# Dealing out DVE work and summing v in longer bursts in a windowed-attention and Fourier-mixing kernel

## The chip, the cores and the metric

The kernel runs on one core of one Trainium2 chip. The time is device time of one execution in microseconds; the time before is the median of three executions. One further execution was profiled, and all rows of a profile come from that one. The core has a matrix engine (TensorE, PE in the profile, with its weight loads as PEld), a vector engine (VectorE, DVE), a scalar engine (ScalarE, ACT), GpSimd (POOL), and the queue SP (SyncE), which issues nearly all DMAs here. Each engine takes its own instructions in order and waits for the others by semaphores.

## The reference

```python
g = sigmoid((x * gate_w).sum(-1))                  # x: 2048 x 512
a = x @ dft_hid_re.T;  b = x @ dft_hid_im.T        # 512 x 512 each
y = dft_seq_re @ a - dft_seq_im @ b                # 2048 x 2048 each
q, k, v = heads(x @ wqkv)                          # 32 heads of 16
p = softmax(mask(q @ k.T / 4))                     # 0 <= i - j < 256
out = g * y + (1 - g) * ((p @ v) @ wo)
```

All inputs and outputs are float32. There are two branches over the same 2048 rows: a Fourier mixing, which is dense matmuls alone, and an attention in which each row sees the 256 rows up to itself. A gate per row mixes the two.

## The kernel before

**Dense stream.** A generator, `dense`, yields one matmul of 512 columns at a time: the projections to q and k (`qk_proj`, four groups `g` of heads, rows named `dqk`), to v (`v_proj`, `dv`) and to the Fourier branch (`ab_proj`, `dab`), then the large products with `cr` and `ci` (`c_part`, L446, `dc`), last the product with `wo` (L669). Every dense operand is kept as a high and a low part in the type float32r, and each product is three matmuls (`TERMS`: high by high, high by low, low by high). Twelve matmuls make one projected tile. An operand is split by `split`: L80 copies the high part, L81 subtracts it for the low part. `split_raw` does this for a whole weight, in four DVE operations of 512 columns one behind the other. A tile that a projection made is split as it leaves PSUM (L84 on ACT, L86 or L88 on DVE) into a tile `hl`, of which there are three, and stored to `qk_scr` or `ab_scr` in HBM.

**Attention.** 128 blocks of 64 rows (4 groups of heads by 32), each with four pairs of heads `p`. `s_pair` makes the scores of block n (L325), DVE adds the mask and finds the minimum of the negated scores (L327), ACT takes the exponentials only for their sum `l` (L330). 20 blocks later (`LAG`) `t_pair` makes the transposed scores of block k = n - 20 with the maxima built in (L388), ACT writes their exponentials into a tile `pt` (L389; four tiles), GpSimd cuts the edges of the window (L394, L398), and `pv` sums v with them (L415, rows named `o`, float32, 32 columns of the array for each pair). The maxima and the sums of 8 blocks are turned from columns to rows by `ml_rows`: one matmul with a float32 identity (L337), then DVE work (L340 to L344) and small DMAs; `m_ring` loads the maxima back. `make_pad` (L308, L310) writes the block's weights. `v_load` and `v_spread` bring v for four blocks at a time into one of two `vpad` tiles (L378 on GpSimd).

**Order.** The order on TensorE is written out by hand in the last loop: for each block and pair a score matmul, dense matmuls, a transposed score matmul, dense matmuls. `fill` adds to a quota and takes that many from the dense stream, which gives 4 x `FILL` dense matmuls per block: 12 for the first 20 blocks (`FILL_FIRST` 3.0), 14 while there are projections left (`FILL_PROJ` 3.5), 14.4 later (`FILL_SEQ` 3.6). Every third block, behind pair 2, `pv` is called for three blocks at once (a burst), and `ml_rows` behind it when eight blocks of sums are complete. On the other engines a scheduler sets the order from its own estimate; `behind` keeps an instruction behind the last one marked on the named engines, and `late` does so for ACT and DVE.

**Buffers.** PSUM has four banks for `s`, `t` and the turned rows (`ps_a`), two for `o`, two for dense products. Raw weights and rows of x have two tiles `raw`, their splits three each of `hi` and `lo`; a load into a tile waits on SP, with every later DMA of that queue behind it.

**End.** After the loop `attention_done` loads and splits `wo`. The rest of the dense stream follows, with the products of `wo` between blocks of 48 `dc` matmuls; `wo_prep` loads and splits (`os`, L78 and L81) the attention's output for them.

## Time and profile before

| | before |
|---|---|
| median of 3 runs | 869.55 us (868.85 to 870.48) |
| profiled execution, whole | 873.39 us |
| its span, first to last instruction | 871.3 us |
| TensorE busy | 860.5 us, 99% |
| DVE busy | 611.3 us, 70% |
| ACT busy | 580.9 us, 67% |
| POOL busy | 384.6 us, 44% |
| granted TensorE clock, mean | 0.998 |
| DMA | 157.87 MB, mean 181 GB/s |

Engine rows of the page give busy time, share of the span and the number of instructions. The chain is the work that ended last, followed back from the last instruction. A row of the timeline has its start, its length, the engine, the line, and what it writes and reads, with shapes and count; in square brackets the idle time before it and what ended that. A matmul's length holds a tail that the next one overlaps, so the rate is read from one start to the next. A row of the waits has the engine and its line, the one waited for, the total in us, the count and the longest. A group of instructions has its busy time, the mean of one in ns, and the idle time before. Busy time by stretch has the stretch, its length, and for PE, PEld, DVE, ACT and POOL the busy time with the number of instructions.

### The profile page before, as it was taken

The page shows a single profiled execution, that of the slowest core. Times are in us where ns is not written, and L with a number is a line of the kernel's source. Part 1 is how long each engine was busy: PE and PEld are TensorE (multiplying, and loading weights), DVE is VectorE, ACT ScalarE, POOL GpSimd, SP SyncE. Part 2 cuts the span into 40 slices and gives each one's busy share as a digit, 9 for nine tenths or more (in the row PEclk, how much of TensorE's full clock was granted, in tenths as well). Part 3 has the DMA queues.
Part 4 walks back from the last instruction along what each step waited for, and adds up shares of the span by engine and source line. Part 5 has one row for each costly group of instructions (what it writes and reads, how often), then busy time and mean ns, then how long its engine had stood idle before and what let it go on. Part 6 is the DMA issues. An engine that isn't in the chain of part 4 may idle for free.

```text
span 871.3 us, 17146 instructions
## 1 busy us (share of the span) xinstructions
PE 860.5 (99%) x5160; PEld 690.3 (79%) x5160; DVE 611.3 (70%) x1974; ACT 580.9 (67%) x1793; POOL 384.6 (44%) x1067
## 2 busy tenths in 40 slices
PE   8999999999999999999999999999999999999998
PEld 6888778787877778878788887878778787788886
DVE  4588987667878987878787777788876444564431
ACT  4388799888897987878788777877776454111110
POOL 9100054545444756656456566554546665200000
PEclk9999999999999999999999999999999999999999
DMA  6875796464749436644445354599944333485541
GB/s 229 266 226 155 248 262 197 153 214 158 241 158 289 130 105 225 172 130 135 134 131 170 105 163 133 156 349 256 329 148 159 123 118 114 130 263 192 189 145 48
DMA packets 93132, 157.87 MB, mean 181 GB/s; under 512 B 27120, under 2 KB 36080, under 8 KB 93040
## 3 DMA queue, kind: packets, MB, share of 16 engines
q1 hardware_dynamic: 92288, 155.61, 56.5%
q10 hardware_dynamic: 752, 1.18, 0.4%
q8 instruction: 40, 0.66, 0.3%
q14 instruction: 52, 0.43, 0.2%
HBM read 106.69 MB, written 50.07 MB: 180 GB/s over the span
## 4 chain that ended last, share of the span: by engine, by line
PE 92%; DVE 3%; DMA 2%; ACT 1%; issue 1%; SPq 0%; DVEq 0%; ACTq 0%
PE dc L446 40%; PE dab L266 9%; PE s L325 8%; PE o L415 8%; PE dqk L244 8%; PE t L388 8%; PE t L669 5%; PE dv L266 4%; DVE sm L327 1%; PE s L232 1%; DMA raw<-x 1%; ACT sm L330 1%; DMA ring<-qk_scr 1%; PE s L337 1%; DMA pt<-xT 0%
## 5 line engine op out<-in xcount | busy, mean ns | idle before, releaser
L446 PE MATMUL dc<-big,hi 128*128 128x512 f32 x1024 | 355.4, 395 | 0.0
L394 POOL TENSOR_SCALAR_AFFINE_SELECT pt<-pt 64x128 f32<-64x128 f32 x512 | 191.9, 375 | 276.4 <-ACT pt L389 261.2
L330 ACT ACTIVATE sm<-sm,ml 128x320 f32<-128x320 f32 (+4 forms) x512 | 277.3, 543 | 49.4 <-DVE ml L327 48.0
L327 DVE CUSTOM_DVE_ANT_0 sm<-s,mask 128x320 f32<-128x320 f32 (+4 forms) x512 | 230.7, 462 | 82.7 <-PE s L325 62.5
L389 ACT ACTIVATE pt<-t 128x320 f32<-128x320 f32 (+4 forms) x512 | 208.7, 412 | 89.8 <-PE t L388 86.2
L446 PEld LDWEIGHTS dc<-big,hi 128*128 128x128 f32 x1024 | 186.3, 188 | 32.6 <-issue 2.4
L446 PE MATMUL dc<-big,lo 128*128 128x512 f32 x512 | 201.6, 394 | 0.0
L398 POOL TENSOR_SCALAR_AFFINE_SELECT pt<-pt 64x128 f32<-64x128 f32 x448 | 161.9, 361 | 0.1
L325 PE MATMUL s<-ring,pad 128*128 128x320 f32 (+4 forms) x512 | 159.0, 310 | 0.9 <-DVE ml L327 0.5
L388 PE MATMUL t<-ring,pad 128*128 128x320 f32 (+4 forms) x512 | 155.1, 303 | 1.6 <-DVE ml L327 0.9
L310 DVE TENSOR_SCALAR pad<-ring,half 96x256 fp32r<-96x256 f32 x384 | 121.6, 358 | 24.2 <-PE t L388 22.0
L325 PEld LDWEIGHTS s<-ring,pad 128*128 128x128 f32 x512 | 96.0, 188 | 36.6 <-issue 7.4
L388 PEld LDWEIGHTS t<-ring,pad 128*128 128x128 f32 x512 | 96.1, 188 | 21.6 <-DVE ml L327 2.6
L446 PEld LDWEIGHTS dc<-big,lo 128*128 128x128 f32 x512 | 96.3, 188 | 10.6
L81 DVE TENSOR_TENSOR lo<-raw,hi 128x512 fp32r<-128x512 f32 x146 | 99.6, 712 | 1.4 <-PE dc L446 1.3
L330 ACT ACTIVATION_READ_ACCUMULATOR sm<-sm,ml 128x1 f32 x512 | 98.8, 193 | 0.0
L266 PE MATMUL dab<-hi,big 128*128 128x512 f32 x256 | 90.9, 396 | 0.0
L244 PE MATMUL dqk<-big,hi 128*128 128x512 f32 x240 | 86.7, 394 | 0.6 <-DVE hl L86 0.5
L80 DVE CAST hi<-raw 128x512 fp32r<-128x512 f32 x142 | 58.6, 453 | 38.3 <-PE dc L446 37.1
L415 PE MATMUL o<-pt,vpad 128*32 128x320 f32 (+4 forms) x1408 | 73.8, 351 | 0.0
L378 POOL COPY vpad<-vr 64x256 f32<-64x256 f32 x64 | 26.0, 405 | 91.1 <-DMA vr<-v_scr 72.0
L308 ACT ACTIVATE pad<-ring,half 96x256 fp32r<-96x256 f32 x128 | 64.1, 500 | 0.0
(82 smaller groups left out, 780.3 us busy)
## 6 DMA issues: line engine op xcount, KB each, us to landing
qk_scr<-hl SPq DMA_DIRECT2D x32, 512.0 KB
ring<-qk_scr SPq DMA_DIRECT2D x32, 512.0 KB
raw<-cr SPq DMA_DIRECT2D x32, 512.0 KB
raw<-ci SPq DMA_DIRECT2D x32, 512.0 KB
ab_scr<-hl SPq DMA_DIRECT2D x20, 512.0 KB
big<-ab_scr SPq DMA_DIRECT2D x20, 512.0 KB
r_scr<-ev SPq DMA_DIRECT2D x36, 256.0 KB
ev<-r_scr SPq DMA_DIRECT2D x36, 256.0 KB
```

Source lines behind the costliest of these rows:

```text
L244: nc.tensor.matmul(ps, w[a][:, c:c + 128], XT[dk, ss][:, b], start=n == 0, stop=n == 11)
L266: nc.tensor.matmul(ps, XT[dk, ss][:, a, c * 128:(c + 1) * 128], wh[b], start=n == 0, stop=n == 11)
L310: nc.vector.tensor_scalar(dst, src, half[:96, h:h + 1], None, op0=OP.mult)
L325: nc.tensor.matmul(ps[:, :w], PAD[0, n][:, p], ring[1][:, p, k0:k0 + w], start=True, stop=True)
L327: mark("dve", nc.vector.tensor_tensor_reduce(out=sm[:, :w], in0=ps[:, :w], in1=mask[:, WIN - w:], scale=1.0, scalar=3e38, op0=OP.add, op1= ...
L330: mark("act", nc.scalar.activation(sm[:, :w], sm[:, :w], AF.Exp, bias=nm[:, c], scale=-1.0, accum_out=l[:, c]))
L388: nc.tensor.matmul(ps[:, :w], PAD[1, n][:, p], ring[0][:, p, q0:q0 + w], start=True, stop=True)
L389: nc.scalar.activation(pt[:, p, :w], ps[:, :w], AF.Exp, scale=-1.0)
L394: nc.gpsimd.affine_select(a, a, pattern=[[0, 2], [1, 64]], compare_op=OP.is_ge, fill=0.0, base=0, channel_multiplier=-1)
L398: nc.gpsimd.affine_select(a, a, pattern=[[0, 2], [-1, 64]], compare_op=OP.is_gt, fill=0.0, base=0, channel_multiplier=1)
L415: nc.tensor.matmul(OT[g, sb][32 * p:32 * p + 32, q - sb * 512:e - sb * 512], v2[:, p], pt[:, p, q - q0:e - q0], start=first, stop=kb == 8 ...
L446: nc.tensor.matmul(ps, w[a][:, i % 8 * 128:i % 8 * 128 + 128], ab[SC[i]][:, b], start=i == ends[0] and a + b == 0, stop=i == ends[1] and a ...
```

## The change

Six things are changed.

- `FILL_PROJ` goes from 3.5 to 4.0 and `FILL_SEQ` from 3.6 to 3.8: 16 and 15.2 dense matmuls per block.
- Weight splits (`split_soon`), the splits of x (`x_job`) and the gate products are put on a list `jobs`. `job`, called behind every matmul of a projection, takes one from it at the third and the ninth of its twelve matmuls. The splits of `cr`, `ci` and `wo` stay as they were. Several loads of raw weights move with the splits that free their tiles.
- Once all projections are through, the sums of v go in bursts of five blocks. The tiles `hl` have grown to the size of a `pt` and serve as two more of these (`more`), so there are six; there are two `hl` where there were three.
- v is spread as soon as the sums that read the older `vpad` are issued, in the burst, and the load for the next four blocks follows (`v_next`).
- Turning: `ml_split` splits maxima and reciprocal sums in a high and a low part, `ml_turn` turns both with two float32r matmuls (the identity is float32r now) two blocks later, `ml_rows` takes them on a pair later, `m_ring` three blocks after that. A table, `TURN`, has their places.
- The last loop is one block shorter (`N + LAG + 1`), and the last sums are taken when k reaches N.

```diff
@@ -26,7 +26,7 @@
...
 SWITCH = 4
-FILL_FIRST, FILL_PROJ, FILL_SEQ = 3.0, 3.5, 3.6
+FILL_FIRST, FILL_PROJ, FILL_SEQ = 3.0, 4.0, 3.8
 @with_exitstack
@@ -100,6 +100,20 @@
...
         return hi, lo
+    jobs = []
+    def split_soon(raw):
+        hi = st.tile([P, 1024], F32R, name="hi")
+        lo = st.tile([P, 1024], F32R, name="lo")
+        for c in HALVES:
+            jobs.append(lambda c=c: late(nc.vector.tensor_copy, hi[:, c], raw[:, c]))
+            jobs.append(lambda c=c: late(nc.vector.tensor_sub, lo[:, c], raw[:, c], f(hi[:, c])))
+        return hi, lo
+    def job(n):
+        if n % 6 == 3 and jobs:
+            jobs.pop(0)()
     def load_split(src, act=False):
@@ -154,9 +168,9 @@
...
                                 base=256, channel_multiplier=1)
-    ident = const.tile([P, P], F32, name="ident")
-    nc.gpsimd.memset(ident, 1.0)
-    nc.gpsimd.affine_select(ident, ident, pattern=[[1, P]], compare_op=OP.is_equal, fill=0.0,
+    ident = const.tile([P, P], F32R, name="ident")
+    nc.gpsimd.memset(f(ident[:]), 1.0)
+    nc.gpsimd.affine_select(ident[:], f(ident[:]), pattern=[[1, P]], compare_op=OP.is_equal, fill=0.0,
                             base=0, channel_multiplier=-1)
@@ -218,8 +232,12 @@
     TERMS = ((0, 0), (0, 1), (1, 0))
+    def hl_tile():
+        t = ev.tile([P, NP, WIN], F32R, name="hl", bufs=2)
+        return t.rearrange("p a b -> p (a b)")[:, :1024].rearrange("p (h s) -> p h s", h=2)
     def qk_evict(g, ss, i, ps):
-        hl = ev.tile([P, 2, 512], F32R, name="hl", bufs=3)
+        hl = hl_tile()
         split_psum(hl[:, 0], hl[:, 1], ps, -SCALE if i == 0 else 1.0)
@@ -244,6 +262,7 @@
...
                     n += 1
+                    job(n)
                     if n < 12:
@@ -266,6 +285,7 @@
...
                 n += 1
+                job(n)
                 if n < 12:
@@ -286,7 +306,7 @@
...
         if dst is None:
-            hl = ev.tile([P, 2, 512], F32R, name="hl", bufs=3)
+            hl = hl_tile()
             split_psum(hl[:, 0], hl[:, 1], ps, 1.0 if i == 0 else -1.0)
@@ -311,6 +331,8 @@
...
     ML = {}
+    MH = {}
+    MT = {}
     def s_pair(n, p):
@@ -330,22 +352,35 @@
...
                                          accum_out=l[:, c]))
+    def ml_split(u):
+        ml = ML.pop(u).rearrange("p x c -> p (x c)")
+        MH[u] = at.tile([P, 2, NP * 16], F32R, name="mlh", bufs=1)
+        with behind("dve"):
+            nc.vector.reciprocal(ml[:, 32:], ml[:, 32:])
+            nc.vector.tensor_copy(MH[u][:, 0], ml)
+            mark("dve", nc.vector.tensor_sub(MH[u][:, 1], ml, f(MH[u][:, 0])))
+    def ml_turn(u):
+        hl = MH.pop(u)
+        MT[u] = ps_a.tile([P, 512], F32, name="s", tag="st")
+        for h in range(2):
+            nc.tensor.matmul(MT[u][:64, h * P:h * P + P], hl[:, h], ident, start=True, stop=True)
     def ml_rows(u):
-        ml = ML.pop(u)
-        nc.vector.reciprocal(ml[:, 1], ml[:, 1])
-        pt = ps_a.tile([P, 512], F32, name="s", tag="st")
-        nc.tensor.matmul(pt[:64, :P], ml.rearrange("p x c -> p (x c)"), ident, start=True, stop=True)
-        hl = at.tile([32, 2, 2, 64], F32R, name="mhl", bufs=1)
-        m = pt[:32, :P].rearrange("c (a r) -> c a r", a=2)
-        nc.vector.tensor_scalar(hl[:, :, 0], m, -1.0, None, op0=OP.mult)
-        nc.vector.scalar_tensor_tensor(hl[:, :, 1], m, -1.0, f(hl[:, :, 0]), op0=OP.mult, op1=OP.subtract)
-        ld(m_scr[u].rearrange("x p (j r) -> (p j) x r", r=64), f(hl[:]).rearrange("c a h r -> c (a h) r"))
-        lt = at.tile([64, P], F32, name="lt", bufs=1)
-        nc.vector.tensor_copy(lt[32:64], pt[32:64, :P])
+        pt = MT.pop(u)
+        rows = at.tile([64, 2 * P], F32R, name="mhl", bufs=1)
+        hl = rows[:32].rearrange("c (a h r) -> c a h r", a=2, h=2)
+        lt = f(rows[32:64, :P])
+        m = pt[:32, :2 * P].rearrange("c (h a r) -> c h a r", h=2, a=2)
+        with behind("dve"):
+            nc.vector.tensor_scalar(hl.rearrange("c a h r -> c h a r"), m, -1.0, None, op0=OP.mult)
+            nc.vector.tensor_copy(lt, pt[32:64, :P])
+            mark("dve", nc.vector.tensor_add(lt, pt[32:64, P:2 * P], lt))
+        ld(m_scr[u].rearrange("x p (j r) -> (p j) x r", r=64), f(hl).rearrange("c a h r -> c (a h) r"))
         for a in range(2):
...
             ld(bass.AP(tensor=ls.tensor, offset=ls.offset + a * 512, ap=[[1024, NP], [64, 8], [1, 64]]),
-               lt[32:64, 64 * a:64 * a + 64])
+               lt[:, 64 * a:64 * a + 64])
     def m_ring(u):
@@ -355,6 +390,7 @@
...
     PT = {}
+    more = []
     VR = {}
@@ -382,7 +418,12 @@
...
         if p == 0:
-            PT[n] = at.tile([P, NP, WIN], F32, name="pt", bufs=4)
+            if "proj" in have:
+                more.append(n)
+            if more and (n - more[0]) % 6 < 2:
+                PT[n] = f(ev.tile([P, NP, WIN], F32R, name="hl", bufs=2)[:])
+            else:
+                PT[n] = at.tile([P, NP, WIN], F32, name="pt", bufs=4)
         pt = PT[n]
@@ -492,24 +533,28 @@
...
         yield
+        def x_job(ss, dk):
+            late(split_x, ss, (dk,), ss == 1)
+            if dk % 2 and ss < 3:
+                load_x(ss + 1, dk // 2)
         for ss in range(4):
+            if ss < 3:
+                for dk in range(DK):
+                    jobs.append(lambda ss=ss, dk=dk: x_job(ss + 1, dk))
+                    jobs.append(lambda: None)
             if ss:
                 yield from qk_proj(0, ss, wq0)
+            if ss == 3:
+                w = split_soon(raw)
             for c in range(4):
...
                     have.add(("qk", 0, ss))
-                if ss < 3:
-                    if c in (1, 2):
-                        late(split_x, ss + 1, (2 * c - 2, 2 * c - 1), ss == 0)
-                        if ss < 2:
-                            load_x(ss + 2, c - 1)
-                elif c == 0:
+                if ss == 2 and c == 2:
                     raw = load_raw(wqk[1])
                     wraw = [load_raw(wi[0])]
-                elif c == 2:
-                    w = late(split_raw, raw)
         for g in range(1, NG):
@@ -517,28 +562,27 @@
...
                         wraw.append(load_raw(wi[1]))
-                    elif ss < 3:
-                        if ss == 1:
-                            ws = []
-                        ws.append(late(split_raw, wraw[ss - 1]))
-                        if ss == 1:
-                            raw = load_raw(wqk[2])
+                        ws = [split_soon(wraw[0])]
+                    elif ss == 1:
+                        ws.append(split_soon(wraw[1]))
+                        raw = load_raw(wqk[2])
                 elif g == 2:
...
                         wraw = [load_raw(wr[0])]
+                    elif ss == 1:
+                        nextw = split_soon(raw)
                     elif ss == 2:
-                        nextw = late(split_raw, raw)
                         wraw.append(load_raw(wr[1]))
-                elif ss in (0, 2):
-                    if ss == 0:
-                        ws = []
-                    ws.append(late(split_raw, wraw[ss // 2]))
+                elif ss == 0:
+                    ws = [split_soon(wraw[0])]
+                elif ss == 1:
+                    ws.append(split_soon(wraw[1]))
             if g == 1:
...
                     if sb == 1:
-                        nextw = late(split_raw, raw)
+                        nextw = split_soon(raw)
             if g < 3:
@@ -550,8 +594,7 @@
...
                 if sb > 1:
-                    late(gate, 2 * sb - 4)
-                    late(gate, 2 * sb - 3)
+                    jobs.extend([lambda tb=tb: late(gate, tb) for tb in (2 * sb - 4, 2 * sb - 3)])
         for sc in range(4):
@@ -703,13 +746,21 @@
...
     N = NG * NB
-    maxima = sent = 0
-    taken = []
+    TURN = (8, 1, ml_split), (10, 0, ml_turn), (10, 1, ml_rows), (13, 0, m_ring)
     need(("qk", 0, 0))
...
     need(("v", 5))
-    for n in range(N + LAG + 2):
+    summed, spread = 0, 2
+    def v_next(n):
+        if n < N:
+            for c in range(2):
+                need(("v", n % NB // 2 + c))
+            with behind(*(("sp",) if n < 8 else ())):
+                v_load(n)
+    for n in range(N + LAG + 1):
         if n in (1, 3, 5):
@@ -717,13 +768,12 @@
...
         ring_ahead(n + 1)
-        if -4 <= k < N - 4 and k % 4 == 0:
-            for c in range(2):
-                need(("v", (k + 4) % NB // 2 + c))
-            with behind(*(("sp",) if k < 4 else ())):
-                v_load(k + 4)
-        if -4 <= k and k % 4 == 3:
+        if k in (-4, 0):
+            v_next(k + 4)
+        if k in (-1, 3):
             v_spread(k + 1)
+        if k == 3:
+            v_next(8)
         if n == 0:
@@ -737,17 +787,18 @@
...
             fill(n)
-            if p == 2 and sent < maxima and n >= taken[sent] + 2:
-                m_ring(sent)
-                sent += 1
-            if p == 2 and k % 3 == 0:
-                for j in range(k - 3, k):
-                    if 0 <= j < N:
-                        pv(j)
-                if maxima < 16 and n > 8 * maxima + 8:
-                    ml_rows(maxima)
-                    maxima += 1
-                    taken.append(n)
+            for at_n, at_p, do in TURN:
+                u, j = divmod(n - at_n, 8)
+                if p == at_p and j == 0 and 0 <= u < 16:
+                    do(u)
+            if p == 2 and (k - summed >= (5 if more else 3) or k == N):
+                for j in range(summed, k):
+                    pv(j)
+                summed = k
+                while 4 * spread - 5 < summed and 4 * spread < N:
+                    v_spread(4 * spread)
+                    spread += 1
+                    v_next(4 * spread)
     attention_done()
```

## The prediction

> **What bounds the kernel now.** I read the page first (engines, then the chain that ended last), then the chain in order of time, then the timeline of TensorE in short stretches, the waits, and busy time by stretch.
>
> ```profile
> span 871.3 us, 17146 instructions
> PE 860.5 (99%) x5160; PEld 690.3 (79%) x5160; DVE 611.3 (70%) x1974; ACT 580.9 (67%) x1793; POOL 384.6 (44%) x1067
> ...
> PE 92%; DVE 3%; DMA 2%; ACT 1%; issue 1%; SPq 0%; DVEq 0%; ACTq 0%
> ```
>
> TensorE is busy for 99% of the span and carries 92% of the chain. So time can be won only where a matmul takes longer than its share of a dense stream, and lost only where TensorE starts to wait. The page's means cannot give that share, since neighbouring matmuls overlap; starts can.
>
> ```profile
> 758.84 21.12 PE dc L446 x92
> 779.96 10.99 PE t L669 x48
> ...
> 812.82 10.88 PE dc L446 x48
> ```
>
> 48 matmuls of 512 columns in 10.88 us are 0.227 us each.
>
> ```profile
> 353.71 0.31 PE L325 MATMUL s<-ring,pad 128*128 128x320 f32 x1
> 353.86 0.40 PE L446 MATMUL dc<-big,hi 128*128 128x512 f32 x1
> ...
> 354.47 0.39 PE L446 MATMUL dc<-big,hi 128*128 128x512 f32 x1
> 354.80 1.84 PE L415 MATMUL o<-pt,vpad 128*32 128x192 f32 x48
> 356.56 0.42 PE L325 MATMUL s<-ring,pad 128*128 128x320 f32 x1
> 356.82 0.40 PE L446 MATMUL dc<-big,hi 128*128 128x512 f32 x1
> 357.05 0.40 PE L446 MATMUL dc<-big,lo 128*128 128x512 f32 x1
> ...
> 757.99 0.39 PE L446 MATMUL dc<-big,hi 128*128 128x512 f32 x1
> 758.30 0.54 PE L415 MATMUL o<-pt,vpad 128*32 128x128 f32 x16
> ...
> 759.11 0.40 PE L446 MATMUL dc<-big,lo 128*128 128x512 f32 x1
> ```
>
> A score matmul of 320 columns takes 0.15 us (353.71 to 353.86). The `o` rows are the sums of v. Around them the stream stumbles: from the dense matmul at 354.47 to the second one behind (357.05) are 2.58 us, of which two dense matmuls and a score are 0.60, so the sums of three blocks (960 columns) cost 1.98. The last sums (128 and 64 columns) cost 759.11 - 757.99 - 2 x 0.227 = 0.67. The line through both has 1.71 ns per column and **0.34 us fixed per burst**, whatever its length.
>
> ```profile
> 308.61 1.84 PE L415 MATMUL o<-pt,vpad 128*32 128x256 f32 x48
> 310.38 0.43 PE L337 MATMUL s<-ident,ml 128*64 128x128 f32 x2
> ...
> 310.99 0.39 PE L266 MATMUL dab<-hi,big 128*128 128x512 f32 x1
> ...
> 501.99 0.22 PE L325 MATMUL s<-ring,pad 128*128 128x128 f32 x1
> 502.05 0.44 PE L446 MATMUL dc<-big,hi 128*128 128x512 f32 x1
> 502.33 0.39 PE L446 MATMUL dc<-big,lo 128*128 128x512 f32 x1
> ```
>
> With a turning behind it, the stretch from the burst to the dense matmul is 310.99 - 308.61 = 2.38 us, without one 356.82 - 354.80 = 2.02: the float32 turning (two records) costs **0.36 us**. A float32r matmul of 128 columns takes 0.06 (501.99 to 502.05), and the one behind it is late by 0.28 - 0.23 = 0.05, since its weights aren't covered.
>
> ```profile
> 105.60 0.40 PE L244 MATMUL dqk<-big,hi 128*128 128x512 f32 x1
> 106.52 0.41 PE L388 MATMUL t<-ring,pad 128*128 128x320 f32 x1 [0.52 <-ACT pad L308]
> ...
> 279.05 0.39 PE L266 MATMUL dab<-hi,big 128*128 128x512 f32 x1
> 279.88 0.42 PE L388 MATMUL t<-ring,pad 128*128 128x320 f32 x1 [0.44 <-DVE ml L327]
> ...
> PE t L388 <- DVE ml L327: 0.9, 3, 0.4
> ...
> PEld s L325 <- ACT sm L330: 3.6, 7, 0.5
> PEld s L325 <- DVE ml L327: 3.3, 9, 0.6
> PEld t L388 <- DVE ml L327: 2.6, 6, 0.8
> ```
>
> Third kind: stalls. The first pair of rows is 0.92 us apart where 0.23 would do, the second 0.83. TensorE's own waits give 0.9 us for the costliest group, the weight loads' three largest together 9.5; a load may wait without holding its matmul, so the truth lies between. I take **9 us**, near the upper end, because the two sites shown lose 1.3 us where the bracketed waits say 0.96. All name the evictions of scores by DVE and ACT.
>
> **The change, part by part.** The work on TensorE is otherwise the same: both built orders hold 2,688 dense matmuls behind the 8 of the warming, 1,024 of scores and 704 of sums of v.
>
> 1. Five-block sums. The built order has 31 bursts instead of 43: 12 x 0.34 = **-4.1 us**. The rest of a burst goes by columns and stays. While a burst of five runs (1,600 columns, 1,600 x 1.71 ns + 0.34 = 3.1 us) no scores come, so ACT and DVE drain and must catch up; that belongs to step 3. The six buffers of `pt` and `hl` hold five blocks and the one in work, so the exponentials don't wait. The loads of v are as many as before; GpSimd spreads v one burst ahead; a second spread in a burst waits for its DMA with the masks queued behind it, but the next burst is five blocks away. At nothing; its cover is POOL's 56% idle on the page.
>
> 2. Turning. Sixteen times 0.36 becomes two float32r matmuls: 2 x 0.06 + 0.05 = 0.17. 16 x 0.19 = **-3.0 us**; -1.0 if each of the two took as long as a score of 320 columns, 0.15 (16 x 0.06); -5.8 if the turning vanished. The Trainium skill (FP8 and Floating Point Precision, TensorE Precision Notes) says that true FP32 makes four passes through the array; by passes alone the old turning would be 4 x 0.06 = 0.24, the saving 16 x 0.12 = 1.9 and the whole sum 1.1 us smaller. The rows disagree (0.36), so I keep theirs.
>
> 3. Density and single DVE operations. Per score block 16 dense matmuls instead of 14 while projecting, 15.2 instead of 14.4 later. This moves dense work from behind the attention into it and costs nothing by itself, but gives each quarter block 0.5 x 0.227 = 0.11 us, or later 0.05, more for DVE and ACT.
>
> ```profile
> 45.00:75.00 30.00, 30.00 (x144) 25.33 (x143) 26.12 (x103) 25.48 (x81) 0.00 (x0) 1.00 0.66 209
> 420.00:560.00 140.00, 140.00 (x926) 113.28 (x925) 108.80 (x384) 114.21 (x366) 80.86 (x217) 1.00 0.47 137
> ...
> L81 DVE TENSOR_TENSOR lo<-raw,hi 128x512 fp32r<-128x512 f32 x146 | 99.6, 712 | 1.4 <-PE dc L446 1.3
> L340 DVE TENSOR_SCALAR mhl<-s 32x128 fp32r<-32x128 f32 x16 | 4.5, 279 | 24.8 <-PE s L337 24.8
> ```
>
> Busy columns are PE, PEld, DVE, ACT, POOL. DVE stands at 87% early and 78% late, ACT at 85 and 82, so they keep up on average; the stalls are lumps. A weight split puts four operations in a row ahead of a score's eviction (two of 0.71); dealt out, at most one. DVE's 1.55 us idle per turning (24.8 / 16) goes too. The splits of `cr` and `ci` stay in lumps, and the stalls past 300 us with them. Of 9 us I take 5: **-5 us**, between -9 and 0.
>
> 4. Where the turned rows wait. They take one of the four score banks for a quarter block, and `ml_rows` now stands behind the next score's eviction. The second score behind the turning needs the bank after 3 x 0.15 + 6 x 0.227 = 1.8 us. By then DVE must have evicted a score and done three operations of about 0.28: with matmul and eviction some 0.8 + 0.84, just in time, and in some rounds a later operation of 0.7 is ordered among them. **+1.5 us**, 0.1 per turning; 0 to 16 x 0.5 = 8.
>
> 5. Two `hl` buffers for three. 52 evictions must each wait for the store of the one before the last.
>
> ```profile
> 82.18 5.97 DMA ring<-qk_scr
> ...
> 111.07 0.58 ACT L84 ACTIVATE hl<-dqk 128x512 fp32r<-128x512 f32 x1
> ...
> 119.41 0.62 ACT L84 ACTIVATE hl<-dab 128x512 fp32r<-128x512 f32 x1
> ...
> SPq L56 <- DVE lo L81: 105.9, 48, 10.7
> ```
>
> Evictions two apart come 8.3 us apart here (111.07 and 119.41, with one between). After the change it is 24 dense and some 12 scores, 24 x 0.227 + 12 x 0.15 = 7.3, and its share of a burst. A buffer lives for the eviction (0.58 on ACT, some 0.7 on DVE as in the L81 row) and its DMA: by the nearest row, a load on the same queue, 6 us, so 7.3 too. It fits, except where SP stands before a raw load (2.2 us in the mean). What waits behind `hl` on ACT is the exponentials, and TensorE behind their banks after 1.2 us. **+1.5 us**, 0 to 52 x 0.25 = 13.
>
> 6. Gate products and input splits one at a time: inside step 3. A load of `x` now holds SP up to two job places (12 dense matmuls, about 4 us) longer; behind it stand v and ring loads that are wanted blocks later. At nothing.
>
> 7. The end. Wo's first matmul comes 53 dense matmuls after the last sum, 53 x 0.227 = 12.0 us, where it had 92 (758.84 to 779.96).
>
> ```profile
> 769.21 0.62 ACT L78 CAST os<-ev 128x512 fp32r<-128x512 f32 x1 [16.80 <-DMA ev<-o_scr]
> 769.86 0.69 DVE L81 TENSOR_TENSOR os<-ev,os 128x512 fp32r<-128x512 f32 x1 [3.85 <-ACT os L78]
> ```
>
> The last sums began at 758.30 and took some 0.5, and their first split operand was there at 770.55: 11.8 us, as it stands. The others follow at 0.8 us against 2.7 us of matmul each. At 0, up to +3.
>
> Sum: -4.1 - 3.0 - 5 + 1.5 + 1.5 = -9.1. The profiled execution took 873.39 us (871.3 of span and 2.1 around it), so 864.3 on its scale. The median of the runs, 869.55, lies 3.8 below; I forecast **860.5**.
>
> **The rivals.**
> - Density does nothing: the stalls come from the order on DVE and of `cr`/`ci`, step 3 is 0. 865.5. For: those splits are left as they are. Against: the two sites shown lie in the projections.
> - The bank of the turning (step 4) stalls at 0.4 us each: 16 x 0.3 = +4.8, 865.3. For: the margin is nil. With step 3 at 0 as well it is 870, no change.
> - The other side: the `hl` buffers. If SP's hold of 2.2 us falls on most stores, the buffer lives 9.5 us against about 8, ACT waits 1.5 us and the banks cover 1.2 of it: 0.25 to 0.3 us on TensorE, 52 x 0.25 = 13 instead of 1.5, so 872. It decides from 0.2 us per eviction (10.6 / 52). For: the row of SP's waits. Against: in the stretch shown the queue let the store out in time for 8.3 us.
> - The end is late by 3 us: 863.5.
>
> **How the numbers follow.** Forecast (856 to 864) 0.48; density nothing 0.14; bank 0.10; end late 0.04; bank and density together 0.05; `hl` 0.19. All of step 3, with the turning vanishing, gives 869.55 - 4.1 - 5.8 - 9 = 850.7; I cut the low end at 853, where the forecast's tail is thin, and reach up to 872.5 for `hl`. A change under 0.2% (1.7 us) cannot be told from none here. The first four are faster (0.74, with a little of them ending near no change), bank and density together no change (0.06), `hl` slower (0.20).
>
> **What would show it.** Right: 31 bursts with the same stumble; no L337-like pair of 0.36; gaps at 105 and 279 us gone; `wo` starting at the end without a gap. Wrong: ACT's evictions into `hl` waiting for DMA `qk_scr` or `ab_scr`; the second score behind each turning held by DVE; more PE waits for exponentials after the longer bursts.

## The result and the profile after

The changed kernel takes **873.29 us** in the median of 22 runs (869.89 to 876.73), the kernel before 870.64 us (22 runs beside it, 868.85 to 876.13). The ratio is 1.0027, with a 95% interval of 1.0015 to 1.0038: slower by 0.3%, where 860.5 us and faster was forecast.

The profiled executions point the other way, 869.89 us after (span 868.2) against 873.39 before (871.3), and must not be compared as they stand. Busy time by stretch at the start shows why: first the kernel before, then the changed one (the columns are the stretch, its length, busy time of PE, PEld, DVE, ACT and POOL, the granted TensorE clock, the DMA share, GB/s).

```profile
6.00:12.00 6.00, 4.49 (x11) 3.32 (x12) 5.97 (x11) 4.85 (x10) 6.00 (x4) 0.72 0.64 240
```

```profile
6.00:12.00 6.00, 6.00 (x24) 4.85 (x24) 4.98 (x10) 5.47 (x11) 6.00 (x4) 1.00 0.57 222
```

The profiled execution of before had a clock of 0.72 in this stretch and got through 11 matmuls, where the changed kernel had full clock and 24. I added up the starts of the matmuls: the part until the first projections are done took 9.6 us before and 6.4 us after. Those 3 us are no part of the change: e2 and e3 below have the old start and take 6.5 us for it. So the changed kernel's own trace, taken from its fastest run (869.89 us), is about level with the kernel before (870.64); its other runs are slower.

The page of the changed kernel (its span, the engines, and the chain that ended last):

```profile
span 868.2 us, 17212 instructions
PE 852.6 (98%) x5160; PEld 690.4 (80%) x5160; DVE 614.7 (71%) x2006; ACT 588.3 (68%) x1793; POOL 387.8 (45%) x1067
...
PE 80%; DMA 10%; DVE 7%; issue 2%; ACT 1%; SPq 0%; ACTq 0%; DVEq 0%
```

TensorE's share of the chain fell from 92% to 80%, and DMA's rose from 2% to 10%. TensorE waits more, and behind its waits stand DMAs. The shares alone don't make the loss, though: e1 below, which is faster than the kernel before, has 81% and 9%. The costly rows of the changed kernel's waits (total, count, longest):

```profile
DVE pad L330 <- DMA ring<-qk_scr: 6.5, 3, 2.8
...
DVE ev L466 <- DMA ev<-l_scr: 3.9, 1, 3.9
...
ACT hl L84 <- DMA qk_scr<-hl: 3.4, 1, 3.4
PE dab L285 <- DVE hl L88: 3.3, 1, 3.3
...
ACT hl L84 <- DMA ab_scr<-hl: 1.7, 1, 1.7
```

`ACT hl L84 <- DMA qk_scr<-hl` is an eviction that waits until the store of an earlier one has left its buffer. The kernel before has no such row. The timeline of the changed kernel shows this place, and also a burst and a turning:

```profile
106.73 3.90 SPq L56 DMA_DIRECT2D ring<-qk_scr  x4
110.73 1.27 SPq L56 DMA_DIRECT2D vr<-v_scr  x2
112.59 2.76 SPq L56 DMA_DIRECT2D qk_scr<-hl  x2
...
118.23 0.39 PE L285 MATMUL dab<-hi,big 128*128 128x512 f32 x1
120.51 0.60 ACT L84 ACTIVATE hl<-dab 128x512 fp32r<-128x512 f32 x1 [3.44 <-DMA qk_scr<-hl]
121.14 0.69 DVE L88 SCALAR_TENSOR_TENSOR hl<-dab,hl 128x512 fp32r<-128x512 f32 x1 [1.91 <-ACT hl L84]
121.89 0.50 PE L285 MATMUL dab<-hi,big 128*128 128x512 f32 x1 [3.27 <-DVE hl L88]
...
139.80 0.28 PE L367 MATMUL s<-ident,mlh 128*64 128x128 f32 x2
139.92 0.36 PE L347 MATMUL s<-ring,pad 128*128 128x320 f32 x1
140.12 0.62 PE L285 MATMUL dab<-hi,big 128*128 128x512 f32 x2
...
360.19 0.40 PE L487 MATMUL dc<-big,lo 128*128 128x512 f32 x1
360.52 1.82 PE L456 MATMUL o<-pt,vpad 128*32 128x320 f32 x24
362.15 1.27 PE L456 MATMUL o<-hl,vpad 128*32 128x256 f32 x32
363.55 0.65 PE L487 MATMUL dc<-big,hi 128*128 128x512 f32 x2
...
597.40 0.87 DVE L330 TENSOR_SCALAR pad<-ring,half 96x256 fp32r<-96x256 f32 x3 [2.80 <-DMA ring<-qk_scr]
598.74 0.41 PE L429 MATMUL t<-ring,pad 128*128 128x320 f32 x1 [2.10 <-DVE ml L349]
```

Read the first seven rows from the bottom. TensorE stands from 118.23 + 0.23 to 121.89, 3.4 us, because its next dense product needs a PSUM bank that DVE and ACT have not emptied. ACT could not empty it before 120.51, because both `hl` were still being stored. The older of the two stores (of the eviction at 108.01) was issued at 112.59, since SP was busy with four ring loads and two loads of v, and it left the buffer at 120.5. ACT takes its work in order, so the exponentials waited behind the eviction too.

The burst at 360 us is as forecast: from 360.19 to 363.55, less one dense matmul, are 3.13 us for five blocks (forecast 3.1). The turning is too: two matmuls in 139.92 - 139.80 = 0.12 us, and 0.05 more behind them. At 598.74 TensorE waits for DVE, and DVE for a ring load.

To compare runs I added up the steps from one matmul's start to the next on TensorE, and call what exceeds a step's share by more than 0.115 us a stall. Stalls are 6.1 us in the trace before and 13.2 us after, 3.4 of it at 122 us and 2.3 at 599 us.

### The profile page after: what moved, and what is told of

Same layout as the page of the kernel before. It is cut to its first block, busy times and chain, and to the rows that moved or that the text cites. A ratio compares the mean times of both kernels' runs of the same rounds, so it can differ in the third digit from the quotient of the medians.

```text
span 868.2 us, 17212 instructions
## 1 busy us (share of the span) xinstructions
PE 852.6 (98%) x5160; PEld 690.4 (80%) x5160; DVE 614.7 (71%) x2006; ACT 588.3 (68%) x1793; POOL 387.8 (45%) x1067
## 4 chain that ended last, share of the span: by engine, by line
PE 80%; DMA 10%; DVE 7%; issue 2%; ACT 1%; SPq 0%; ACTq 0%; DVEq 0%
PE dc L487 36%; PE s L347 8%; PE dqk L262 7%; PE o L456 7%; PE t L429 7%; PE dab L285 6%; PE dv L285 5%; DMA ev<-o_scr 2%; DMA out<-ev 2%; DVE sm L349 2%; DMA ring<-qk_scr 2%; DMA qk_scr<-hl 2%; PE t L712 1%; DVE pad L330 1%; DMA ev<-l_scr 1%
## 5 line engine op out<-in xcount | busy, mean ns | idle before, releaser
L435 POOL TENSOR_SCALAR_AFFINE_SELECT pt<-pt 64x128 f32<-64x128 f32 x392 | 144.6, 369 | 233.2 <-ACT pt L430 220.7
L487 PEld LDWEIGHTS dc<-big,hi 128*128 128x128 f32 x1024 | 183.7, 188 | 26.0 <-issue 1.1
L430 ACT ACTIVATE pt<-t 128x320 f32<-128x320 f32 (+4 forms) x392 | 160.5, 412 | 58.8 <-PE t L429 55.3
L330 DVE TENSOR_SCALAR pad<-ring,half 96x256 fp32r<-96x256 f32 x384 | 119.6, 355 | 32.0 <-PE t L429 25.3
L439 POOL TENSOR_SCALAR_AFFINE_SELECT pt<-pt 64x128 f32<-64x128 f32 x344 | 127.6, 371 | 0.0
L81 DVE TENSOR_TENSOR lo<-raw,hi 128x512 fp32r<-128x512 f32 x132 | 90.6, 715 | 0.1
L80 DVE CAST hi<-raw 128x512 fp32r<-128x512 f32 x128 | 52.5, 451 | 25.9 <-PE dc L487 21.8
L435 POOL TENSOR_SCALAR_AFFINE_SELECT hl<-hl 64x128 f32<-64x128 f32 x120 | 44.2, 368 | 55.8 <-ACT hl L430 51.9
L430 ACT ACTIVATE hl<-t 128x320 f32<-128x320 f32 (+4 forms) x120 | 48.9, 410 | 26.3 <-PE t L429 25.1
```

The lines of the kernel that those rows point to most:

```text
L81: nc.vector.tensor_sub(lo, raw, f(hi))
L330: nc.vector.tensor_scalar(dst, src, half[:96, h:h + 1], None, op0=OP.mult)
L430: nc.scalar.activation(pt[:, p, :w], ps[:, :w], AF.Exp, scale=-1.0)
L435: nc.gpsimd.affine_select(a, a, pattern=[[0, 2], [1, 64]], compare_op=OP.is_ge, fill=0.0, base=0, channel_multiplier=-1)
L439: nc.gpsimd.affine_select(a, a, pattern=[[0, 2], [-1, 64]], compare_op=OP.is_gt, fill=0.0, base=0, channel_multiplier=1)
L487: nc.tensor.matmul(ps, w[a][:, i % 8 * 128:i % 8 * 128 + 128], ab[SC[i]][:, b], start=i == ends[0] and a + b == 0, stop=i == ends[1] and a ...
```

## The experiments

My theory was that the two `hl` buffers make the loss. The rival was that the gains themselves were missing: early DVE work, five-block bursts or density that cost what they save. So each part was undone or done alone.

**Three buffers again.** The changed kernel, with three slices of a fixed 12 KB tile as `hl`; the first 10 KB of it also serve the two extra `pt` later.

```diff
...
-        t = ev.tile([P, NP, WIN], F32R, name="hl", bufs=2)
-        return t.rearrange("p a b -> p (a b)")[:, :1024].rearrange("p (h s) -> p h s", h=2)
+        c = len(hl_at) % 3 * 1024
+        hl_at.append(c)
+        return hls[:, c:c + 1024].rearrange("p (h s) -> p h s", h=2)
...
```

> The changed kernel with three `hl` slices again, in one tile of 12 KB that two of the six `pt` also use; all else as changed. Theory 1 (the exponentials and the dense products wait on ACT for the store that frees one of only two `hl`; the profile after has 3.4 and 1.7 us of such waits on ACT and gaps of 3.4 and 0.9 us on TensorE at 122 and 159 us): those waits are gone and the time is 4 to 7 us under the changed kernel's, 866 to 869, so 2 to 5 under the kernel before. Theory 2 (the longer bursts or the denser stream make the stalls, the buffers do not matter): within 1.5 us of the changed kernel's 873.3.

Measured: 867.31 us, ratio to before 0.9966 (0.9952 to 0.998). One buffer turns a loss of 0.3% into a gain of 0.3%: 6.0 us. In the waits of this kernel ACT's evictions wait for TensorE alone, never for a store:

```profile
ACT hl L84 <- PE dqk L266: 6.9, 3, 4.4
...
ACT hl L84 <- PE dab L289: 0.9, 1, 0.9
```

**Two buffers in the kernel before.**

```diff
-        hl = ev.tile([P, 2, 512], F32R, name="hl", bufs=3)
+        hl = ev.tile([P, 2, 512], F32R, name="hl", bufs=2)
```

> The kernel before with two `hl` tiles instead of three, nothing else. In the profile before, the evictions at 111 and 115 us came 8.3 and 7.5 us ahead of the one after next. Theory 1: waits of ACT for stores of `qk_scr` or `ab_scr` appear in the stretch from 85 to 125 us, and the time is 2 to 6 us over the kernel before. Theory 2: within 1 us of it.

Measured: 873.35 us, ratio 1.0035 (1.002 to 1.0049), so 3.0 us. The rows of its waits that before lacks:

```profile
ACT hl L84 <- DMA ab_scr<-hl: 4.2, 2, 2.2
ACT hl L84 <- DMA qk_scr<-hl: 3.7, 2, 2.3
```

The same wait, so it belongs to the buffer count and not to the rest of the change; with the rest of the change it costs twice as much. Part of that doubling is the clock (last section): these runs have the mean clock of the kernel before, those of the change have not.

**The turning alone**, in the kernel before: `ml_split`, `ml_turn`, `ml_rows` and the table `TURN` of the changed kernel, and nothing else of it.

```diff
...
-    maxima = sent = 0
-    taken = []
+    TURN = (8, 1, ml_split), (10, 0, ml_turn), (10, 1, ml_rows), (13, 0, m_ring)
...
-                if maxima < 16 and n > 8 * maxima + 8:
-                    ml_rows(maxima)
...
+            for at_n, at_p, do in TURN:
+                u, j = divmod(n - at_n, 8)
+                if p == at_p and j == 0 and 0 <= u < 16:
+                    do(u)
```

> The kernel before with the new turning alone (split, two float32r matmuls, rows and ring at the places of the changed kernel). Step 2 of the prediction: 3.0 us less on TensorE, so 867.6 where before is 870.6. If the turned rows hold a score bank too long (step 4), the second score behind each turning is late by 0.3 us or more and the time is 870 or above.

Measured: 870.40 us, ratio 1.0002 (0.9994 to 1.0011). Nothing is won, although the turnings and the step behind each take 3.2 us instead of 7.5 in the starts. In the trace of e3 bursts and their edges grow by 2.4 us, and exposed weight loads and stalls by 2.0. Of the 2.4 us 1.5 only changed their place: 14 of the 16 turnings of before stood right behind a burst and held the late step behind it, 0.11 us each. The other 0.9 are one burst, at 119.8 us, that took 2.75 us where before took 1.85. So the turnings themselves saved about 2.8 us in the starts, nearly the 3.0 of the forecast, and as much was lost again at other places. What makes these losses was not tested.

**Three-block bursts to the end**, three buffers, the rest as changed.

```diff
...
-            if "proj" in have:
-                more.append(n)
...
+            PT[n] = at.tile([P, NP, WIN], F32, name="pt", bufs=4)
```

> The changed kernel with bursts of three blocks to the end and with the three `hl` tiles of the kernel before; denser stream, dealt operations and new turning stay. Theory 1: 43 bursts cost 12 x 0.34 = 4.1 us more than in the run with three `hl` slices, the buffer waits are gone: 870 to 872. Theory 2 with the longer bursts as the cause: 867 to 869, under the run with three slices and five blocks. Theory 2 with the denser stream as the cause: 873 or above.

Measured: 868.64 us, ratio 0.9982 (0.9972 to 0.9993). Against e1, five-block bursts are worth 1.3 us by the medians and not 4.1; the intervals of e1 and e4 overlap, so the 1.3 us are not clear of nothing. The 12 fixed costs are saved in the starts (bursts with their edges take 80.3 us in e4 and 76.1 in e1, 4.2 us), but stalls grow: 7.9 us in e4, and 8.7 in e1 once a wait of 2.1 us at 27 us for a load of x, before any burst, is set aside. The rest of the difference is in the end, in weight loads, and in the clock (below).

**Density and dealing, each undone in e1.**

```diff
-FILL_FIRST, FILL_PROJ, FILL_SEQ = 3.0, 4.0, 3.8
+FILL_FIRST, FILL_PROJ, FILL_SEQ = 3.0, 3.5, 3.6
```

> The kernel of e1 (the change with three buffers for the evictions) with the former rates of dense work (3.5 and 3.6 per half-turn of a block for 4.0 and 3.8). Theory A, step 3 of the prediction: density gives DVE and ACT time and is worth about half of step 3's 5 us, so without it 867.3 + 2.5 = 869.8 us. Rival B: the rates only move dense work, the stalls come from the order on DVE and from late loads, and 867.3 stays within 1 us.

```diff
-        if n % 6 == 3 and jobs:
-            jobs.pop(0)()
+        for _ in jobs[:4 if n % 6 == 3 else 0]:
+            jobs.pop(0)()
```

> The kernel of e1 with up to four waiting DVE jobs taken at once, where e1 takes one every six dense matmuls: the splits come in lumps again, the density stays. Theory A, step 3: lumps put four operations in a row ahead of a score's eviction, the stalls return, 867.3 + 2.5 = 869.8 us or more. Rival B: while DVE is busy for 87% of the time before 110 us, the sum of its work counts and not its order, and dealing only moved the stalls; the time stays at 867.3 within 1 us, or falls.

Measured: 874.53 us without the density (1.0049, 1.0034 to 1.0065) and 869.38 us with lumps (0.9995, 0.9981 to 1.001). Density is worth 7.2 us here, more than either theory said; dealing 2.1 us (7.7 and 2.5 when each kernel is set against the runs of before beside it).

**Five-block bursts alone**, in the kernel before, with the shared tile of e1.

```diff
...
-            if p == 2 and k % 3 == 0:
-                for j in range(k - 3, k):
-                    if 0 <= j < N:
-                        pv(j)
+            burst = p == 2 and (k - summed >= (5 if more else 3) or k == N)
+            if burst:
+                for j in range(summed, k):
+                    pv(j)
+                summed = k
...
```

> The kernel before with five-block sums behind the projections (31 bursts for 43) in three buffers of 4 KB that two blocks' exponentials share, the old turning, density and splits kept. Theory A, step 1: 12 x 0.34 = 4.1 us, 870.3 - 4.1 = 866.2 us. Rival B, from e1 against e4: a longer burst leaves more to catch up behind it, and 1.3 us are left, 869.0 us. A third outcome, 870.3 or more, would mean that the longer bursts cost as much in stalls as they save.

Measured: 878.21 us, ratio 1.0096 (1.0078 to 1.0115). The third outcome, and far beyond it. Two rows of its timeline, and its busy time around the second:

```profile
607.58 0.47 PE L403 MATMUL t<-ring,pad 128*128 128x320 f32 x1 [2.36 <-DVE ml L335]
...
624.99 0.61 PE L403 MATMUL t<-ring,pad 128*128 128x320 f32 x1 [6.53 <-DMA ring<-m_scr]
```

```profile
618.00:625.00 7.00, 0.47 (x3) 0.06 (x2) 2.80 (x10) 2.26 (x8) 1.53 (x5) 0.75 0.94 328
625.00:628.60 3.60, 3.60 (x11) 3.08 (x12) 0.50 (x2) 1.42 (x4) 0.15 (x1) 0.55 0.36 98
628.60:635.00 6.40, 6.40 (x34) 5.51 (x33) 5.67 (x17) 4.82 (x15) 4.16 (x12) 1.00 0.11 41
```

The old turning hangs on the bursts. With a burst every five blocks the maxima are turned later, and their rows reach the ring 6.5 us after the transposed scores want them. So the bursts need the turning at places of its own, and this run prices that dependence more than the bursts. The stretches show a second cost: TensorE is granted 0.55 of its clock over the 3.6 us *after* the stall.

**The second pass 18 blocks behind**, in e1.

```diff
-LAG = 20
+LAG = 18
```

> The kernel of e1 with the second pass over the scores 18 blocks behind the first instead of 20. The columns of the ring come free two blocks earlier against their next use, so a load has five blocks for three. Theory A: the stall of 1.7 us at 597 us (DVE waits for a ring load that stands behind six loads of another tensor) goes, and with it about 1 us of the stalls at 418 us, 867.3 - 2.5 = 864.8 us. Rival B: the stalls depend on what happens to fall together, others appear in their place, and 867.3 stays within 1 us.

Measured: 869.54 us, ratio 0.9997 (0.9982 to 1.0012), 2.2 us above e1: theory A fell, and theory B's 1 us was passed as well. No `pad` waits for a ring load any more, but the turned rows are now late. Its wait, and busy time by stretch around it:

```profile
PE t L434 <- DMA ring<-m_scr: 2.0, 1, 2.0
```

```profile
636.00:638.40 2.40, 0.50 (x3) 0.08 (x1) 1.48 (x7) 1.85 (x7) 2.24 (x8) 1.00 0.84 242
638.40:642.40 4.00, 3.89 (x12) 3.31 (x13) 1.24 (x4) 1.95 (x6) 3.13 (x13) 0.57 0.65 216
```

**Density with three-block bursts**: in e4, the rates of e5.

```diff
-FILL_FIRST, FILL_PROJ, FILL_SEQ = 3.0, 4.0, 3.8
+FILL_FIRST, FILL_PROJ, FILL_SEQ = 3.0, 3.5, 3.6
```

> The kernel of e4 (the change with three-block sums to the end and three buffers for the evictions) with the former rates of dense work (3.5 and 3.6). With five-block sums the rates were worth 7.2 us (e1 867.3, e5 874.5). Theory A: density is worth as much whatever the sums, 868.6 + 7.2 = 875.8 us. Theory B: density pays for the longer bursts alone (e7, five-block sums at the old rates, lost 8.3 us on the kernel before), and with three-block sums the time stays at 868.6 within 1 us.

Measured: 872.39 us, ratio 1.0027 (1.0013 to 1.004), 3.8 us above e4 and 2.0 above e3: between the theories. Against e3 it adds the dealing (with the loads of weights, x and v that move along), so at the old density dealing *costs* 2.0 us. Busy time from 86 to 106 us, first of before, then of e3, then of e9:

```profile
86.00:106.00 20.00, 19.89 (x92) 15.60 (x91) 17.87 (x67) 16.01 (x51) 0.79 (x2) 1.00 0.76 237
```

```profile
86.00:106.00 20.00, 18.97 (x91) 15.09 (x90) 18.88 (x69) 15.38 (x48) 1.60 (x5) 1.00 0.56 196
```

```profile
86.00:106.00 20.00, 18.40 (x83) 13.76 (x82) 18.97 (x69) 14.47 (x45) 0.79 (x2) 1.00 0.56 188
```

TensorE gets 83 matmuls through in e9, against 91 in e3 and 92 in before. DVE is at 95%, against 94% and 89%, so it has no room left in either e3 or e9. With the dealing both splits of `wi` fall into this stretch: eight operations on raw weights in e9, six in e3, four in before. These blocks have 12 dense matmuls in all three kernels, since `FILL_FIRST` was left alone. The starts of the scores, whose order is the same in e3 and e9, tell where the trace of e9 falls behind: 1.2 us at 25 us (a wait for a load of x), 2.0 us between 74 and 124 us, and 0.3 us net in all the rest. That the two added operations make the 2.0 us was not tested; in e9 DVE also waits 1.6 us for ring loads in the stretch, in e3 not at all.

**Towards a faster version**, all from e1: the second pass 19 blocks behind (`LAG = 19`, as in the diff above); the load of the reciprocal sums a burst earlier (the diff below); both.

```diff
...
+        if kb % 8 == 2:
+            rl = ev.tile([P, 512], F32, name="ev")
+            ls = l_scr[g * 4 + kb // 8]
+            ld(rl, bass.AP(tensor=ls.tensor, offset=ls.offset, ap=[[512, 2 * NP], [0, 16], [1, 512]]))
+            RL[g, kb // 8] = rl
         if kb % 8 == 7:
...
-            rl = ev.tile([P, 512], F32, name="ev")
+            rl = RL.pop((g, sb))
```

> The kernel of e1 with the second pass 19 blocks behind the first. With 20 a ring load came 1.7 us late at 597 us, with 18 (e8) the turned rows of the maxima came 2.0 us late at 638 us and the clock halved behind that. Theory A: with 19 both have time (one block is 4.6 us), both stalls go, 867.3 - 2 = 865.3 us. Theory B: stalls of this kind are moved by any shift of the order, and the time stays at 867.3 within 1 us or rises.

> The kernel of e1 with the load of the reciprocal sums (into `ev`, ahead of the multiplication of o) issued with the third block of eight instead of the eighth, a burst earlier. In the trace of e1 DVE waits 4.3 us for it at 412 to 417 us with a score's eviction behind it, and TensorE 1.2 + 0.3 us. Theory A: this stall goes, 867.3 - 1.5 = 865.8 us. Theory B: one of five `ev` buffers is held for a burst more, other users of `ev` wait, and the time stays at 867.3 within 1 us or rises.

> The kernel of e1 with both: 19 blocks, and the sums' load a burst earlier. Theory A: the savings add, 867.3 - 3.5 = 863.8 us. Theory B: no more than the better of the two alone.

Measured: 863.30 us with 19 blocks (0.9924, 0.9904 to 0.9943), 865.16 us with the earlier load (0.9934, 0.992 to 0.9948), 868.36 us with both (0.998, 0.9965 to 0.9995). The first two beat both kernels; their intervals overlap, so neither is shown to be the better one. With 19 blocks no stall above 1.4 us is left in the trace, and neither a ring load nor the sums' load has a row among its waits. The savings don't add: with both, a stall of 1.4 us at 564 us appears that neither alone had, and one of 1.6 us at 593 us, where the earlier load alone has 1.3. What makes them was not followed further.

## Why the prediction was wrong

The runs form a ladder from the kernel before to the changed one, each step the difference of the medians, each taken against the kernel before of its own runs:

| | us against before | this step |
|---|---|---|
| turning (e3) | +0.1 | +0.1 |
| and dealing (e9) | +2.1 | +2.0 |
| and density (e4) | -1.7 | -3.8 |
| and five-block bursts (e1) | -3.0 | -1.3 |
| and two `hl` for three (the change) | +2.7 | **+5.7** |

By their intervals the steps of dealing, density and `hl` are clear of noise, those of the turning and the five-block bursts are not. The size of a step depends on its place: density is worth 7.2 us with long bursts, and dealing *gains* 2.1 us once the density is there (e6). The sum was off by 11.7 us (-9.1 forecast, +2.7 measured): 4.2 of them are the `hl` buffers, 3.2 density and dealing, 2.8 the bursts, 1.6 the turning and its bank together.

- **Step 5, the `hl` buffers, is the step that failed**: +1.5 us was forecast, +5.7 measured, enough to turn a gain into a loss. I reckoned with one life for all 52 stores, 7.3 us, against evictions two apart at 7.3 or more. In the changed kernel's trace the median life of a buffer, from the eviction's start to the store's landing, is 5.1 us, so "it fits" held for most; but 10 of 52 live longer than 7.3, the longest 12.5 (108.01 to 120.49). That one had to wait 2.9 us on SP and then 7.9 us for its transfer. I had put the transfer at 6 us by one load. The trace before already spoke against "it fits":

```profile
113.83 3.86 SPq L56 DMA_DIRECT2D qk_scr<-hl  x2
```

The first of these two stores belongs to the eviction at 111.07 and landed at 122.79 (the last count on its semaphore). The eviction at 119.41, which I took for the proof that the queue let the store out in time, began 3.4 us before that, and could only because there was a third buffer. With two it must wait: at this very eviction, the first of `dab`, the changed kernel waits 3.4 us. In all, 11 of the 52 lives in the trace before are over 7.3 us, and five stores land after the next eviction but one has begun. I had read when evictions come, and not when their stores land. The `hl` rival named the right wait and, at 872 us, nearly the right time, but as a small loss at every eviction. The trace of the changed kernel shows two waits on ACT, of 3.4 and 1.7 us, and no others; they hold TensorE for 3.4 and 0.9 us. About 1.9 of the 5.7 us are clock (last section). The rival's 13 us were too many; its time came out by luck, because the gains beside it were too large.

- **Step 1, five-block sums**: the 0.34 us per burst held (31 bursts, 3.13 us for five blocks), and 4.2 us are gone from the starts. At the end 1.3 us are left by the medians (e1 against e4), not clear of nothing. I had said that DVE's and ACT's catching up belonged to step 3 and gave it no price.
- **Step 2, the turning**: 0.17 us each was right, and about 2.8 of the 3.0 us are saved in the starts, but nothing reached the end (e3: +0.1). I gave no price to what a new place of the turning does to the order around it: one longer burst, exposed weight loads and stalls took as much.
- **Step 3, density and dealing**: -5 forecast, -1.8 measured together. The 9 us of stalls that I took were too many: by the starts the trace before has 6.1, and the first gap shown waited for ACT's `pad`, which is no eviction. The gaps at 105 and 279 us are gone from the changed kernel's trace, but others of 0.7 and 0.8 us are there, at 94 and 291 us. The density did what was said: in the starts of e9 stalls of 3.4 us lie between 279 and 309 us, in e4 0.9. Dealing gained where the density rose (e6). In e9 it cost most between 74 and 124 us, where DVE is nearly full without it (94% in e3 from 86 to 106 us); I had read 87% of DVE as "keeps up on average" without asking which splits would be dealt into that stretch.
- **Step 4, the bank of the turned rows**: +1.5 forecast; nearly nothing seen. In e3 one of the sixteen turnings, at 298 us, has scores 0.3 and 0.6 us late behind it, which wait for ACT and not for DVE; in the changed kernel two turnings have a later score 0.3 and 0.2 us late.
- **Step 7, the end**: the last products wait 0.6 us at 842 us for DVE to add the rows of `r`, within the 0 to 3 given.
- **The scale.** Setting the sum against one profiled execution's 873.39 us and shifting by 3.8 was sound; but "the stalls" were also read from that one trace, and can cost more than their length, as the last section shows.

## What to carry to other kernels

Size a buffer by the longest life of its contents, not by the mean: the store behind it shares a queue with bursts of loads, and a wait of an in-order engine holds all that engine's later work. A trace with a buffer to spare shows no wait for a store, but it does show when each store lands; hold that against the eviction that will need the buffer. A cost that is gone from the starts is not yet gone from the end: make the edit alone before counting it as saved. An edit that deals work out moves it in time as well: look up which stretch it falls into, and whether the engine there has anything left.

## What the runs showed of the hardware

Stalls can cost more than their length, through the clock. In e7 and e8 the granted clock is 0.55 to 0.57 in the 3.6 to 4.0 us behind waits of 2.4, 6.5 and 2.0 us, which is 3.2 to 3.4 us at half clock each time ((1 - 0.57) x 4.0 / 0.5, for one). The wait at 607 us, by stretch in e7:

```profile
604.80:607.50 2.70, 0.42 (x3) 0.07 (x1) 2.03 (x7) 0.45 (x2) 1.49 (x4) 1.00 1.06 225
607.50:611.50 4.00, 3.92 (x12) 3.29 (x13) 3.91 (x13) 1.46 (x4) 0.60 (x3) 0.57 1.02 378
```

The changed kernel's own trace has waits of 3.4 and 2.1 us, and full clock behind both; the stretch behind the longer one:

```profile
121.80:126.00 4.20, 4.11 (x23) 3.33 (x27) 3.06 (x10) 4.17 (x14) 2.81 (x10) 1.00 0.56 211
```

What decides is where a wait falls. In the traces the clock changes only on a grid of 3.41 us, whose place differs from run to run (in e7 it changes at 607.79, 611.21, 621.45 and 628.27 us). Here are the grid's windows with the longest idle time of TensorE, which is 3.41 us less its busy time, and both windows of the change's longest wait, each with the clock granted in the window behind it. The row of before is the slow start of its profile.

| trace | window | idle in it | clock behind it |
|---|---|---|---|
| e7 | 621.45 to 624.86 | 3.41 us | 0.50 |
| e7 | 618.03 to 621.45 | 2.99 | 0.50 |
| e7 | 604.38 to 607.79 | 2.36 | 0.50 |
| before | 5.18 to 8.59 | 2.20 | 0.50 |
| e8 | 635.28 to 638.69 | 2.00 | 0.50 |
| e1 | 23.62 to 27.03 | 1.83 | 1.00 |
| the change | 120.09 to 123.50 | 1.80 | 1.00 |
| the change | 116.68 to 120.09 | 1.47 | 1.00 |

In all fourteen traces, between the first clock on record and the last matmul, no window with 1.83 us of idle time or less has half clock behind it, and every one with 2.00 or more has. The change's wait of 3.4 us was cut nearly in the middle by the grid, and neither half was enough; laid a little earlier or later on it, one half would have been, by these figures. That this is what lowers the clock of its other runs is not shown, since only one of its runs was profiled.

That rests on one run of each kernel. Over all runs, the mean granted clock of each run gives an estimate of the time lost, (1 - clock) x time, which takes in half clock during a wait and is so an upper one:

| | runs | mean clock | lost to the clock | the rest |
|---|---|---|---|---|
| before (beside e1 to e4) | 31 | 0.9994 | 0.5 us | 869.8 us |
| e2, before with two `hl` | 8 | 0.9994 | 0.5 | 873.0 |
| e3, turning alone | 11 | 0.9995 | 0.4 | 870.0 |
| the change | 22 | 0.9965 | 3.0 | 870.4 |
| e1, three `hl` | 12 | 0.9988 | 1.1 | 866.3 |
| e5, old density | 9 | 0.9973 | 2.3 | 871.8 |
| e7, before with five-block bursts | 6 | 0.9937 | 5.6 | 872.6 |
| e10, 19 blocks | 6 | 0.9987 | 1.2 | 863.1 |
| e12, both | 12 | 0.9972 | 2.5 | 866.2 |

The last column is the mean time of the runs less the loss. So of the 6.0 us between the change and e1, about 1.9 are clock and 4.1 the rest, the waits themselves above all; and most of what the change loses against before is clock, by this estimate 2.5 us. The clock of the 22 runs of before beside the change is not on record; the value used is that of the 31 others. The change's own runs go the same way: the eight with a clock of 0.998 or more have a mean of 871.3 us, as before has beside them (871.2), and the six with 0.995 or less one of 875.7. With two `hl` alone, in e2, the clock stays, and its 3.0 us are waits.

The Trainium skill (TensorE: Matmul & The Clock Gate, Part 1: The HAM clock gate) says that a window of about 3.4 us, which runs freely, decides the clock, and that it halves after an idle window. The length and the free-running grid agree with the traces here. The idle time doesn't: in e8 a window with 2.00 of its 3.41 us idle was enough.
